# Seven products instead of eight for the first product of chunk 7 and half of chunk 8 of a fused attention and MoE kernel, its gate on GpSimd, x and w_in in fp16

## The chip, the cores and the metric

The kernel runs on one core of one Trainium2 chip. Its engines are TensorE (PE, with its weight loads as PEld), VectorE (DVE), ScalarE (ACT), GpSimd (POOL) and SyncE (SP, which here only issues DMAs). The metric is the device time of one execution in microseconds, the median of several; lower is better.

## The reference

Block-wise causal attention for 8 batches and 8 heads, 576 positions of 64 numbers each, and behind it a two-layer network with a gate. Inputs and output are float32.

```python
scores = scale * np.matmul(q, k.transpose(0, 1, 3, 2))      # scale = 1/8
mask = block_i >= block_j                                   # blocks of 64 positions
attn = softmax(where(mask, scores, -1e9))
x = (attn @ v).transpose(0, 2, 1, 3).reshape(B * S, H * D)  # 4608 x 512
h = x @ w_in                                                # 512 x 2048
g = h * (1.0 / (1.0 + np.exp(-beta * h)))
return g @ w_out                                            # 2048 x 512
```

## The kernel before

**Who decides the order.** The kernel is written as a list of operations (`P.op`), each with the engines that may run it, an estimated duration, what it depends on, the buffers ("tiles") that it holds, and a priority. When the program is made, `Plan.schedule` runs these through a list scheduler: whenever an engine is free it takes, among the operations whose dependencies have ended by the estimates and for which buffers are free, the one with the lowest `prio`. The result is a fixed order for every engine's queue; on the chip each engine works its queue in that order and waits on semaphores. The estimates are `mm(n)` for a matmul of n columns, `act_t(n)` for ScalarE, `dve_t(n)` for VectorE, and plain numbers for GpSimd. PSUM has eight banks of 512 float32 columns; a "P1" tile is one bank, a "PP" tile (attention) a pair.

**Attention.** For each batch and each pair of heads: q and k are loaded (SP queue), cast to bf16 on GpSimd (L625, L665), transposed (PE at L634, later by DMA), multiplied (L708), put through Exp on ScalarE (L724, L736), zeroed where masked (VectorE, L730, L732) and multiplied with v (L764; v is cast on GpSimd at L574). VectorE divides by the row sums into `xq` (L776, L783), and `xq` is transposed into `xT`, by PE and a copy for the first three batches (L813, L821, L823) and by DMA for the rest (L800). `xT` holds x transposed, four blocks of 128 features by up to 2560 rows, in bf16, used as a ring.

**The network.** It goes over nine chunks of 512 rows (r = 0 to 8; chunk 7 begins at row 3584, chunk 8 at 4096). Each chunk has two products.

The first product (L1000) makes 16 blocks of 128 hidden units: for block j four matmuls, over the four blocks of features, of 128x128 weights from `w_in` on 512 columns of `xT`, into one bank. ScalarE takes tanh of it with the scale beta/2 (L1010), and VectorE forms (tanh + 1) times h from the same bank into `gT` in fp16 (L1014), which is 2 h sigmoid(beta h); the factor 2 is taken out at the end.

```python
o = P.op("PE", 4 * mm(512), fh, deps=xd + [win[j // 4]], tiles=[ph, tg], lat=4 * mm(512) + 170,
         mode="full", prio=1000 + 100 * r + j)
```

The second product is, for chunks 1 to 8 (`FAST`), already done in seven products instead of eight (Strassen's way, Winograd's form): `gT` is seen as 2x2 quarters (row half by half of the hidden units), `w_out` likewise, and sums and differences of quarters are multiplied (`fast`, L921, 128x256 matmuls in fp16). VectorE makes these sums (L885, two SBUF inputs; those of `w_out` once, L865). Three of the results run through one bank: ScalarE copies it out (L942), the next product adds into the same bank, and so on; VectorE adds the other banks (L945, and L936 in the last chunk). The outputs go to DRAM through the ACT queue, in the last chunk through SP.

The priorities interleave the second product of chunk r with the first product of chunk r+1: its first two steps stand behind the first product of its own chunk, and the others between the blocks of the next chunk.

```python
prio=1000 + 100 * r + (16 + 0.1 * k if fin or k < 2 else 103 + 16 / 12 * (k - 2))
```

`gT` has two buffers, so the first product of chunk r+1 can begin when the second product of chunk r-1 has ended. Chunk 8 has nothing behind it: its second product runs alone.

**Buffers.** Most of SBUF is taken. The staging buffers of q and k (`ST`, `S4`), of v (`Vs`), the cast copies (`QKn`, `Vn`), the transposed ones (`QKT`) and the exponentials (`E`) are used until the attention of the last batch is done.

**Start.** GpSimd builds two 128x128 identities (L458 to L463), constants in `Vn` and `E`, and then turns to the casts and to the loads of `w_in` and `w_out`, which convert from float32 on the way (L502, L507). Until 50 us TensorE fills pauses with matmuls on constants (L523, L525).

Of the kernel before, what the change touches and what calls it, by code (L numbers as in the profile page):

```python
# [4 lines left out]
ACT = mybir.ActivationFunctionType  # L5
ALU = mybir.AluOpType
f32 = mybir.dt.float32
# [6 lines left out]
NF = 2048  # L14
# [345 lines left out]
def bass_blockwise_causal_attn__then__act_swish_beta_kernel(  # L360
# [10 lines left out]
    with es:  # L371
        def sb(name, shape, dt):
            return es.enter_context(nc.sbuf_tensor(name, shape, dt))
# [7 lines left out]
        JOIN = (2,3,4,5,6,7)  # L381
        NO = 4
        FAST = range(1, NRC)
        RX = 5 * RC
        OV = sb("OV", [128, 5120], f32)
        ST = [sb(f"ST{i}", [128, 36, 64], f32) for i in range(2)]
        STh = [s[:, 18 * i:18 * i + 18] for s in ST for i in range(2)]
        ST6 = [s[0:96].rearrange("p t d -> p (t d)")[:, 768 * i:768 * i + 768].rearrange("p (h j d) -> p h j d", h=2, j=6)
               for s in ST for i in range(3)]
        Vs = [sb("Vs0", [128, 5, 8, 64], f32), OV[:, 2560:5120].rearrange("p (t h d) -> p t h d", t=5, h=8)]  # L390
        OVh = OV[:].bitcast(f16).rearrange("p (s j n) -> p s j n", s=5, j=8)
        TW = {k: OVh[:, k - 2] for k in (2, 3, 4)}
        SW = {k: OVh[:, k + 1] for k in (2, 3)}
        QKn = [sb(f"QKn{i}", [128, 2, 2, 768], bf16) for i in range(NQ)]
        Vn = [sb(f"Vn{i}", [128, 5, 8, 66], bf16) for i in range(NQ)]
        QKT = [sb(f"QKT{i}", [128, 2, 2, 640], bf16) for i in range(3)]
        Ef = [sb(f"E{i}", [128, 3200], bf16) for i in range(NE)]
        gT = [sb(f"gT{i}", [128, NJ, RC], f16) for i in range(2)]

        Ef.append(gT[1][:].bitcast(bf16).rearrange("p j n -> p (j n)")[:, 0:3200])  # L400
        E3 = [e[:, 0:3072].rearrange("p (c h n) -> p c h n", c=3, h=2) for e in Ef]
        E4 = [e[:, 3072:3136] for e in Ef]
        inv = [sb(f"inv{i}", [128, 10], f32) for i in range(4)]
        xq = [sb(f"xq{i}", [128, 5, 128], bf16) for i in range(3)]
        xq.append(gT[1][:].bitcast(bf16).rearrange("p j n -> p (j n)")[:, 3200:3840].rearrange("p (i n) -> p i n", i=5))
        xT = sb("xT", [128, 4, RX], bf16)
        identF = sb("identF", [128, 128], f32)
        identB = sb("identB", [128, 128], bf16)
        w_in = sb("w_in", [128, 4, NF], bf16)
        w_out = sb("w_out", [128, NJ, DM], f16)  # L410
        beta = sb("beta", [128, NJ], f32)
        th = [sb(f"th{i}", [128, RC], f32) for i in range(3)]
# [3 lines left out]
        PS = es.enter_context(nc.psum_tensor("PS", [128, 8, 512], f32))  # L416
        PSb = PS[:].rearrange("p b n -> p (b n)").bitcast(bf16).rearrange("p (b n) -> p b n", b=8)

        identW = identF[:].bitcast(bf16)
        NFILL, TFILL = 400, 50000.0  # L420
        P = Plan()
# [2 lines left out]
            P.slots(c, n)  # L424
        P.slots("S4", 4)
        P.slots("XX", 1)

        def mm(n):
            return max(n / 2.4 + 3, 55.0)

        def act_t(n, ptr=0):
            return 0.833 * n + 93 + 93 * ptr

        def dve_t(n):
            return (n + 125) / 0.96

        LAG = 1.5
        def pr(u):
            b, c = divmod(u, NPAIR)
            return u if b < 1 else 10 * u if b < 2 else 994 + 100 * (b - LAG) + 4.9 * c  # L440
# [11 lines left out]
        def xq_(tx):  # L452
            return 3 if tx.cls == "XX" else tx.slot

        def mk(fn):
            return lambda g, e: fn(g)
# [6 lines left out]
        c4 = P.op("POOL", 430, mk(lambda g: g.affine_select(  # L463
            out=identB[:], in_=identB[:], compare_op=ALU.not_equal, fill=1.0, base=0,
            pattern=[[-1, 128]], channel_multiplier=1)), deps=[c3], prio=-10)
        c2.same, c4.same = [c1], [c3]
        cw = P.op("POOL", 100, mk(lambda g: g.memset(warm[:, 0:1], 0.0)), prio=-20)
        wa = P.op("ACT", 1500, mk(lambda g: g.activation(warm[:, 1:2], warm[:, 0:1], ACT.Exp)), deps=[cw], prio=-60)
        ones, vzero = [], []
# [131 lines left out]
        for u in range(NU):  # L601
# [208 lines left out]
            def fx(g, e, tx=tx, px=px):  # L810
                for i in range(5):
                    r = 128 if i < 4 else 64
                    z = g.transpose(PSb[:, px.slot, 128 * i:128 * i + r], xq[xq_(tx)][0:r, i, :], identB[0:r, 0:r])  # L813
                return z

            xp = P.op("PE", 5 * 66, fx, deps=nrm, tiles=[tx, px], lat=5 * 66 + 170, mode="full", prio=pr(u)+.5 + 5 * (b < 1))

            def fy(g, e, px=px, c=c, b=b):
                for t0, n, x0 in pieces(b):
                    if e == "ACT":  # L820
                        z = g.activation(xT[:, c, x0:x0 + n], PSb[:, px.slot, t0:t0 + n], ACT.Copy)  # L821
                    else:
                        z = g.tensor_copy(xT[:, c, x0:x0 + n], PSb[:, px.slot, t0:t0 + n])  # L823
                return z
            xt.append(P.op("ACT" if u in (2, 3) else "DVE", 600 if u in (2, 3) else 520, fy, deps=[xp], tiles=[px], prio=0))

# [44 lines left out]
        def fast(r, row, tg, gs):  # L871
# [114 lines left out]
            else:  # L986
                store(ou, 1, 0, evac(Y, ou, p4 + [u2], add=ou), rest=1500.0 if r < NRC - 2 else 0.0)

        for r in range(NRC):
            row = RC * r  # L990
            b0, b1 = row // S, (row + RC - 1) // S
            xd = [xt[4 * b + c] for b in range(b0, b1 + 1) for c in range(4)]
            tg = P.tile("gT")
            gs, hs = [], []
            for j in range(NJ):
                ph, tt = P.tile("P1"), P.tile("th")

                def fh(g, e, ph=ph, j=j, row=row):
                    for c in range(4):
                        z = g.matmul(PS[:, ph.slot, :], w_in[:, c, 128 * j:128 * j + 128], xT[:, c, row % RX:row % RX + RC],  # L1000
                                     start=(c == 0), stop=(c == 3))
                    return z

                o = P.op("PE", 4 * mm(512), fh, deps=xd + [win[j // 4]], tiles=[ph, tg], lat=4 * mm(512) + 170,
                         mode="full", prio=1000 + 100 * r + j)

                hs.append(o)

                def fs(g, e, ph=ph, tt=tt, j=j):
                    return g.activation(th[tt.slot][:], PS[:, ph.slot, :], ACT.Tanh, scale=beta[:, j:j + 1])  # L1010
                a = P.op("ACT", act_t(512, 1), fs, deps=[o, bC], tiles=[ph, tt], lat=act_t(512, 1) + 93, prio=0)

                def fg(g, e, ph=ph, tt=tt, tg=tg, j=j):
                    return g.scalar_tensor_tensor(out=gT[tg.slot][:, j, :], in0=th[tt.slot][:], scalar=1.0,  # L1014
                                                  in1=PS[:, ph.slot, :], op0=ALU.add, op1=ALU.mult)
                gs.append(P.op("DVE", dve_t(512), fg, deps=[a] + (spare.users + spare_x.users if r == 1 else []), tiles=[ph, tt, tg], prio=0))

            for b in range(B):
                if any((S * b + a) // RC - RX // RC == r for a in (0, S - 1 if b < XB else 639)):
                    for c in range(4):  # L1020
                        xt[4 * b + c].deps += hs

            if r in FAST:
                fast(r, row, tg, gs)
                continue

            for w, d0, d1 in [(w, 0, DM) for w in range(4)]:
                po, to = P.tile("P1"), P.tile("ost")


                parts = [(4 * a, 4 * a + 4) for a in range(4)]
                o = None
                for j0, j1 in parts:
                    def fo(g, e, po=po, tg=tg, w=w, j0=j0, j1=j1, d0=d0, d1=d1):
                        for j in range(j0, j1):
                            z = g.matmul(PS[:, po.slot, 0:d1 - d0], gT[tg.slot][:, j, 128 * w:128 * w + 128],  # L1036
                                         w_out[:, j, d0:d1], start=(j == 0), stop=(j == NJ - 1))
                        return z

                    n = (j1 - j0) * mm(d1 - d0)  # L1040
                    was = o
                    o = P.op("PE", n, fo, deps=gs[j0:j1] + wout[j0 // 4:(j1 + 3) // 4],
                             tiles=[po, tg], lat=n + 170, mode="full",
                             prio=1000 + 100 * r + (16 + w + 0.01 * j0 if w == 0 else
                                                     103 + 5.33 * (w - 1) + 1.33 * j0 / 4))
                    o.after = was
                    plain.append(o)

                def fv2(g, e, po=po, to=to, n=d1 - d0):
                    if e == "ACT":  # L1050
                        return g.activation(ost[to.slot][:, 0:n], PS[:, po.slot, 0:n], ACT.Copy, scale=0.5)
                    return g.tensor_scalar(out=ost[to.slot][:, 0:n], in0=PS[:, po.slot, 0:n], scalar1=0.5,
                                           scalar2=None, op0=ALU.mult)
                x = P.op("ACT", act_t(d1 - d0) + 80, fv2, deps=[o], tiles=[po, to], lat=act_t(d1 - d0) + 160, prio=0)

                def fd(g, e, to=to, row=row, w=w, d0=d0, d1=d1):
                    return [g.dma_start(out[row + 128 * w:row + 128 * w + 128, d0:d1], ost[to.slot][:, 0:d1 - d0])]
                P.op("ACT", 500, fd, deps=[x], tiles=[to], xfer=900, dma=["d_ost", to], prio=-1)
# [71 lines left out]
```

The softmax here doesn't subtract the row's maximum and nothing guards it: scores larger than these inputs give would overflow.

## Time and profile before

| what | value |
|---|---|
| runs | 334.65, 335.12, 332.92 us; median 334.65 |
| span of the profiled execution, first to last instruction | 330.9 us |
| TensorE, matmuls | 323.5 us busy, 98% |
| VectorE, ScalarE, GpSimd | 221.8, 212.6 and 84.6 us busy |
| first product (L1000) | 576 matmuls |
| second product by seven (L921) | 896 matmuls |
| granted TensorE clock, mean | 0.999 |
| last attention matmul (L764) ends | 262.1 us |
| chunk 7's first product | 267.3 to 288.0 us, mixed with chunk 6's second |
| chunk 8's first product | 292.5 to 314.2 us, mixed with chunk 7's second |
| chunk 8's second product | 314.2 to 328.2 us |

The profiled execution's time is known by its span only; the times of the runs also hold what lies around it, so they stand 2.0 to 4.2 us above the span. A row of the profile gives line, engine, operation, output and inputs, count, then busy time and the mean of one in ns, and last the idle time of the engine before such operations with what ended it. Matmuls overlap, so that the mean of one is longer than its share of the time. In the chain that ended last a piece is given by its start, its length and the instructions in it. In the table of stretches the columns are start and end, length, then busy time and count of PE, PEld, DVE, ACT and POOL, the granted clock, and the DMAs.

### The profile page before, as it was taken

To read this page: it belongs to the slowest core of one execution; us is meant where nothing else is said; L and a number is where in the kernel's file an instruction comes from. 1 tells how busy PE (TensorE), PEld (TensorE's weight loads), DVE (VectorE), ACT (ScalarE), POOL (GpSimd) and SP (SyncE) were. 2 spreads that over 40 slices of the span, in tenths; PEclk is the share of its full clock that TensorE was granted. 3 is DMA by queue.
4 is the path that set the end of the run, shared out by engine and by line. 5 is a ranking of instruction groups with operands and counts; after the bars stand their busy time and mean duration, and the time that the engine had idled before them with its cause. 6 is when DMAs were issued, how large, how long until landed. Compare 5 with 4: busy or idle time off the path is not lost.

```text
span 330.9 us, 7510 instructions
## 1 busy us (share of the span) xinstructions
PE 323.5 (98%) x3145; PEld 204.2 (62%) x3089; DVE 221.8 (67%) x448; ACT 212.6 (64%) x324; POOL 84.6 (26%) x127
## 2 busy tenths in 40 slices
PE   7998999999999999999999999999999999999996
PEld 4574455445586457754765666576566766666685
DVE  4747875679754897358966695678467685666742
ACT  2876974297558886768657866974975555544521
POOL 7665081073073044104621530320000000000000
PEclk9999999999999999999999999999999999999999
DMA  7999999999999999979999999974102310110023
GB/s 214 229 239 234 192 234 198 187 293 200 202 268 190 207 247 198 229 158 216 204 176 224 199 240 214 200 152 80 35 34 40 92 45 34 60 37 32 3 95 127
DMA packets 154993, 53.41 MB, mean 161 GB/s; under 512 B 139072, under 2 KB 154448, under 8 KB 154960
## 3 DMA queue, kind: packets, MB, share of 16 engines
q1 hardware_dynamic: 141200, 40.19, 63.9%
q0 software_dynamic: 5568, 4.36, 8.3%
q10 hardware_dynamic: 8192, 8.39, 8.1%
q8 instruction: 24, 0.39, 0.5%
q14 instruction: 9, 0.07, 0.1%
HBM read 36.71 MB, written 9.44 MB: 139 GB/s over the span
## 4 chain that ended last, share of the span: by engine, by line
PE 92%; ACT 2%; DMA 2%; issue 1%; DVE 1%; SPq 1%; POOL 0%
PE PS L1000 38%; PE PS L921 30%; PE PS L708 9%; PE PS L764 8%; PE PS L1036 4%; DMA ST<-in_k_dram 2%; PE PS L525 1%; PE PS L813 1%; ACT E L724 1%; PE PS L634 1%; ACT xq L788 1%; SPq L618 1%; ACT th L1010 0%; POOL QKn L625 0%; DVE xq L783 0%
## 5 line engine op out<-in xcount | busy, mean ns | idle before, releaser
L1000 PE MATMUL PS<-xT,w_in 128*128 128x512 bf16 x576 | 136.6, 379 | 0.1
L1010 ACT ACTIVATE th<-PS,beta 128x512 f32<-128x512 f32 x144 | 96.5, 699 | 59.8 <-PE PS L1000 59.1
L1014 DVE SCALAR_TENSOR_TENSOR gT<-th,PS 128x512 f16<-128x512 f32 x144 | 95.1, 681 | 31.7 <-ACT th L1010 31.1
L724 ACT ACTIVATE E<-PS 128x1024 bf16<-128x1024 f32 x93 | 92.1, 1028 | 27.0 <-PE PS L708 27.0
L1000 PEld LDWEIGHTS PS<-xT,w_in 128*128 128x128 bf16 x576 | 53.4, 98 | 55.5 <-DVE gT L1014 1.8
L921 PE MATMUL PS<-w_out,gT 128*128 128x256 f16 x512 | 63.1, 273 | 0.0
L921 PEld LDWEIGHTS PS<-w_out,gT 128*128 128x128 f16 x512 | 49.0, 98 | 12.1 <-issue 1.5
L574 POOL CAST Vn<-Vs 128x640 bf16<-128x640 f32 (+1 forms) x28 | 21.6, 770 | 94.3 <-DMA Vs<-in_v_dram 93.1
L665 POOL CAST QKn<-ST 128x640 bf16<-128x640 f32 x48 | 36.7, 764 | 25.1 <-DMA ST<-in_q_dram 12.9
L708 PE MATMUL PS<-QKT 64*128 64x320 bf16 (+4 forms) x328 | 36.4, 297 | 0.4 <-ACT E L736 0.2
L764 PEld LDWEIGHTS PS<-Vn,E 128*128 128x128 bf16 x930 | 30.9, 97 | 3.9 <-issue 0.4
L942 ACT ACTIVATE ost<-PS 128x512 f32<-128x512 f32 x32 | 19.4, 606 | 21.5 <-PE PS L921 21.5
L921 PE MATMUL PS<-OV 128*128 128x256 f16 x256 | 31.9, 273 | 0.0
L764 PE MATMUL PS<-Vn,E 128*128 128x65 bf16 x930 | 31.8, 193 | 0.0
L708 PEld LDWEIGHTS PS<-QKT 64*128 64x128 bf16 (+1 forms) x328 | 13.4, 96 | 26.4 <-issue 11.6
L921 PEld LDWEIGHTS PS<-OV 128*128 128x128 f16 x256 | 24.2, 98 | 5.8 <-issue 1.1
L783 DVE TENSOR_TENSOR xq<-PS,inv 128x640 bf16<-128x640 f32 x30 | 24.6, 822 | 0.7
L885 DVE TENSOR_TENSOR OV<-gT 128x1024 f16<-128x1024 f16 x32 | 23.8, 753 | 1.1 <-PE PS L921 0.6
L730 DVE MEMSET E<- 64x64 uint32 x62 | 6.9, 112 | 22.5 <-ACT E L724 20.4
L945 DVE SCALAR_TENSOR_TENSOR ost<-PS,ost 128x512 f32<-128x512 f32 x22 | 15.1, 688 | 8.7 <-PE PS L921 6.2
L921 PE MATMUL PS<-OV,gT 128*128 128x256 f16 x128 | 16.1, 273 | 0.0
L1036 PE MATMUL PS<-w_out,gT 128*128 128x512 f16 x64 | 15.5, 380 | 0.0
(65 smaller groups left out, 176.2 us busy)
## 6 DMA issues: line engine op xcount, KB each, us to landing
out_dram<-ost ACTq DMA_DIRECT2D x32, 256.0 KB, 3.8
ST<-in_q_dram SPq DMA_DIRECT2D x12, 576.0 KB, 5.4
ST<-in_k_dram SPq DMA_DIRECT2D x12, 576.0 KB, 7.6
Vs<-in_v_dram SPq DMA_DIRECT2D x24, 256.0 KB, 4.3
ST<-in_q_dram SPq DMA_DIRECT2D x8, 288.0 KB, 6.3
ST<-in_k_dram SPq DMA_DIRECT2D x8, 288.0 KB, 6.5
w_in<-in_moe_w_in_dram POOLq DMA_DIRECT2D x4, 512.0 KB, 10.5
w_out<-in_moe_w_out_dram POOLq DMA_DIRECT2D x4, 512.0 KB, 9.5
```

The costliest lines, as they stand in the source:

```text
L574: return g.tensor_copy(Vn[t.slot][:, 0:n, g0:g1, 0:64], Vs[ts.slot][:, 0:n, g0:g1, :])
L665: return g.tensor_copy(QKn[tn.slot][:].rearrange("p a w n -> p (a w n)")[:, 640 * (2 * a + w):][:, 0:640] .rearrange("p (t h d) -> p t h d ...
L708: z = g.matmul(o, QKT[tqk.slot][r, uu % 2, 1, 128 * t + y:128 * t + m + y], x)
L724: return g.activation(E3[es_(te)][:, g0, :, :], PS[:, ps.slot:ps.slot + 2, :], ACT.Exp, scale=0.125)
L764: z = g.matmul(o, eblk(te, t, i, h), Vn[Tv.slot][:, t, 2 * c + h, 0:65], start=(t == 0), stop=(t == i))
L783: return g.tensor_tensor(xq[xq_(tx)][:].rearrange("p i (h d) -> p h i d", h=2), both(pv, 0, 64), x, ALU.mult)
L885: return P.op("DVE", dve_t(SZ * HC / 2), mk(lambda g: g.tensor_tensor(fo(), fx(), fy(), op)), deps=deps, tiles=tiles, prio=prio)
L921: x = g.matmul(PS[:, pw.slot, HM * w:HM * w + HM], fa()[:, j, 128 * w:128 * w + 128], fb()[:, j, :], start=first and (pair or w == 0) and ...
L1000: z = g.matmul(PS[:, ph.slot, :], w_in[:, c, 128 * j:128 * j + 128], xT[:, c, row % RX:row % RX + RC], start=(c == 0), stop=(c == 3))
L1010: return g.activation(th[tt.slot][:], PS[:, ph.slot, :], ACT.Tanh, scale=beta[:, j:j + 1])
L1014: return g.scalar_tensor_tensor(out=gT[tg.slot][:, j, :], in0=th[tt.slot][:], scalar=1.0, in1=PS[:, ph.slot, :], op0=ALU.add, op1=ALU.mult)
L1036: z = g.matmul(PS[:, po.slot, 0:d1 - d0], gT[tg.slot][:, j, 128 * w:128 * w + 128], w_out[:, j, d0:d1], start=(j == 0), stop=(j == NJ - 1))
```

## The change

For chunk 7 (all 16 blocks of hidden units) and chunk 8 (blocks 0 to 7) the first product, too, is done in seven products instead of eight, by a new function `first`. A group is four blocks f: two neighbours i = 0, 1 from each half of eight blocks (chunk 7's groups 0 and 2 cover blocks 0 to 7, groups 4 and 6 blocks 8 to 15). x is seen as 2x2 quarters (256 rows by 256 features), w_in of the group likewise (256 features by 256 hidden units). Each of the seven products has four matmuls of 256 columns.

- Sums and differences of quarters of `w_in` are made once, on GpSimd (`first_weights`, eight operations of 128x1024 in fp16, priority 500, after the last cast of q and k). Those of x are made by VectorE at the beginning of each of the two chunks (four operations).
- The results are put together in float32 in SBUF (`C4`): ScalarE copies a bank out three times a group (`copy`), VectorE adds three banks (`plus`) and copies one. Each holds 2h. Both the combined tiles and those behind them lie in buffers that the attention has used (`ST`, `Vs`, `QKn`, `Vn`, `E`, `QKT`), so chunk 7's products wait for the attention's last use of them.
- The gate becomes ScalarE's Sigmoid from SBUF into `TH` (seven buffers), and a multiplication of `TH` with `C4` on GpSimd into `gT`. The other blocks keep Tanh and the gate on VectorE.
- x (`xq`, `xT`) and `w_in` are fp16 instead of bf16; the transposes on PE need a third identity, in fp16, which GpSimd builds at the start.

```diff
+        F1 = {7: (0, 2, 4, 6), 8: (0, 2)}
...
-        xT = sb("xT", [128, 4, RX], bf16)
+        xT = sb("xT", [128, 4, RX], f16)
...
-        w_in = sb("w_in", [128, 4, NF], bf16)
+        identH = sb("identH", [128, 128], f16)
+        w_in = sb("w_in", [128, 4, NF], f16)
...
+        for c, n in (("T4", 2), ("C4", 9), ("TH", 7)):
+            P.slots(c, n)
...
+        c5 = P.op("POOL", 260, mk(lambda g: g.memset(identH[:], 0.0)), prio=-3)
+        c6 = P.op("POOL", 430, mk(lambda g: g.affine_select(
+            out=identH[:], in_=identH[:], compare_op=ALU.not_equal, fill=1.0, base=0,
+            pattern=[[-1, 128]], channel_multiplier=1)), deps=[c5], prio=-3)
...
+        def first_weights():
+            old = users("ST", "S4") + win
+            a = [[A(f, k) for k in range(2)] for f in range(2)]
+            for k, x, y, op, d in ((1, a[1][0], a[1][1], ALU.add, ()), (3, a[0][0], a[1][0], ALU.subtract, ()),
+                                   (2, SI[1], a[0][0], ALU.subtract, (1,)), (4, a[0][1], SI[2], ALU.subtract, (2,))):
+                si[k] = []
+                for c in range(2):
+                    z = P.op("POOL", 2400, mk(lambda g, o=SI[k], x=x, y=y, c=c, op=op: g.tensor_tensor(
+                        o[:, c], x[:, c], y[:, c], op)), deps=old + [q for i in d for q in si[i]], prio=500)
...
+        def first(r, row, tg, xd):
...
+            dead = users("QKn", "QKT", "Vs", "V", "E") if r == min(F1) else []
...
+                t[k] = P.op("DVE", 400, mk(lambda g, k=k, a=a, b=b, op=op: g.tensor_tensor(TX[tx.slot][k], a(), b(), op)),
+                            deps=xd + dead + [t[i] for i in d], tiles=[tx], prio=0.4)
...
+            for j in F1[r]:
+                Z, W, Y = (P.tile("P1") for _ in range(3))
+                ca, cb = P.tile("C4"), P.tile("C4")
+                at = [1000 + 100 * r + 2 * j]
+
+                def prod(ps, fa, fb, deps, tiles, start, j=j):
+                    def f(g, e):
+                        for i in range(2):
+                            for c in range(2):
+                                z = g.matmul(PS[:, ps.slot, 256 * i:256 * i + 256],
+                                             fa()[:, c, j // 4, 128 * (j % 4 + i):128 * (j % 4 + i) + 128], fb()[:, c, :],
+                                             start=start and i == 0 and c == 0, stop=i == 1 and c == 1, skip_group_check=True)
...
+                    n = 4 * mm(256)
+                    o = P.op("PE", n, f, deps=deps, tiles=[ps, tg, *tiles], lat=n + 170, mode="full", prio=at[0])
+                    at[0] += 0.5
...
+                p1 = prod(Z, lambda: A(0, 0), lambda: X(0, 0), xd + win + dead, [], True)
+                z1 = copy(Z, ca, 0, [p1])
+                p2 = prod(W, lambda: A(0, 1), lambda: X(1, 0), [p1], [], True)
+                c11 = plus(W, ca, 0, [p2, z1])
+                p7 = prod(Y, lambda: SI[3], lambda: TX[tx.slot][3], [t[3], *si[3]], [tx], True)
+                p6 = prod(Z, lambda: SI[2], lambda: TX[tx.slot][2], [t[2], *si[2], z1], [tx], False)
+                u2 = copy(Z, cb, 0, [p6])
+                p5 = prod(Z, lambda: SI[1], lambda: TX[tx.slot][1], [t[1], *si[1], u2], [tx], False)
+                u4 = copy(Z, cb, 1, [p5])
+                c22 = plus(Y, cb, 1, [p7, u4])
+                p3 = prod(Z, lambda: SI[4], lambda: X(1, 1), [u4, *si[4]], [], False)
+                c12 = P.op("DVE", dve_t(512), lambda g, e, Z=Z, ca=ca: g.tensor_scalar(
+                    out=C4[ca.slot][:, :, 1], in0=pair(Z), scalar1=2.0, scalar2=None, op0=ALU.mult),
+                           deps=[p3], tiles=[Z, ca], prio=0)
+                p4 = prod(Y, lambda: A(1, 1), lambda: TX[tx.slot][4], [t[4], c22, *win], [tx], False)
+                c21 = plus(Y, cb, 0, [p4, u2])
+                for i in range(2):
+                    for f, c, d in ((j + i + j // 4 * 4, ca, [c11, c12]), (j + i + j // 4 * 4 + 4, cb, [c21, c22])):
+                        tt = P.tile("TH")
+                        a = P.op("ACT", act_t(512, 1), lambda g, e, tt=tt, f=f, c=c, i=i: g.activation(
+                            TH[tt.slot], C4[c.slot][:, i].rearrange("p h n -> p (h n)"), ACT.Sigmoid, scale=beta[:, f:f + 1]),
+                            deps=d + [bC], tiles=[c, tt], lat=act_t(512, 1) + 93, prio=0)
+                        gs[f] = P.op("POOL", 1250, lambda g, e, tt=tt, f=f, c=c, i=i: g.tensor_tensor(
+                            gT[tg.slot][:, f, :], TH[tt.slot], C4[c.slot][:, i].rearrange("p h n -> p (h n)"), ALU.mult),
+                            deps=[a, *d], tiles=[c, tt, tg], prio=0)
...
-            for j in range(NJ):
+            if r in F1:
+                gs, hs = first(r, row, tg, xd)
+            for j in [j for j in range(NJ) if gs[j] is None]:
```

## The prediction

> **What bounds the kernel now.** I began with the page: engine shares, the forty slices, the chain that ended last.
>
> ```profile
> span 330.9 us, 7510 instructions
> ...
> PE 323.5 (98%) x3145; PEld 204.2 (62%) x3089; DVE 221.8 (67%) x448; ACT 212.6 (64%) x324; POOL 84.6 (26%) x127
> ...
> POOL 7665081073073044104621530320000000000000
> ...
> PE 92%; ACT 2%; DMA 2%; issue 1%; DVE 1%; SPq 1%; POOL 0%
> ```
>
> TensorE is the bound: it works 98% of the span, it is 92% of the chain, and the change touches stretches in which it never pauses. GpSimd has nothing to do in the last 110 us. A microsecond of TensorE work removed near the end is therefore a microsecond of time, but only if the other engines deliver no later than before.
>
> Next the pieces of the chain (start, length, what), because a matmul's own mean includes overlap with the next one, and only back-to-back runs give its true rate:
>
> ```profile
> 267.32 5.18 PE PS L1000 x24
> ...
> 314.16 13.99 PE PS L921 x128
> ```
>
> A 512-column matmul of the first product takes 5.18/24 = 0.216 us, a 256-column matmul of the second product 13.99/128 = 0.1093 us. Two of the small ones cost 0.219, so halving the width costs 1%, although each has its own weight load (98 ns by the L921 row, hidden beneath the matmul).
>
> Then the stretches of chunk 7's and chunk 8's first products (us, then PE, weight load, DVE, ACT, POOL busy):
>
> ```profile
> 262.95:288.12 25.17, 25.17 (x170) 16.39 (x169) 17.82 (x28) 13.39 (x20) 0.00 (x0) 1.00 0.10 29
> 288.12:314.16 26.04, 26.04 (x178) 17.24 (x177) 17.59 (x27) 13.39 (x20) 0.00 (x0) 1.00 0.12 41
> 314.16:330.90 16.74, 13.97 (x128) 12.20 (x126) 6.17 (x11) 3.08 (x5) 0.00 (x0) 0.99 0.32 111
> ```
>
> TensorE is full in the first two, ScalarE half busy, GpSimd empty. The third is chunk 8's second product, alone; the change leaves it as it is.
>
> **The change, part by part.**
>
> *Matmuls.* Four blocks of 128 hidden units took 16 matmuls of 512 columns, 16 x 0.216 = 3.45 us. They become seven products of 4 matmuls of 256 columns, 28 x 0.1093 = 3.06 us. That saves 0.39 us a group; chunk 7 has four groups and chunk 8 two, so 6 x 0.39 = **2.36 us** at the most. The 28 weight loads take 28 x 0.098 = 2.74 us, still under the matmuls. fp16 for bf16 changes no size: the fp16 rate above is the bf16 rate for twice the columns. The transposes, copies and casting loads that now carry fp16 keep their bytes, so I cost them at nothing.
>
> *ScalarE.* Rows for the operations that a group will use:
>
> ```profile
> L1010 ACT ACTIVATE th<-PS,beta 128x512 f32<-128x512 f32 x144 | 96.5, 699 | 59.8 <-PE PS L1000 59.1
> ...
> L942 ACT ACTIVATE ost<-PS 128x512 f32<-128x512 f32 x32 | 19.4, 606 | 21.5 <-PE PS L921 21.5
> ...
> L945 DVE SCALAR_TENSOR_TENSOR ost<-PS,ost 128x512 f32<-128x512 f32 x22 | 15.1, 688 | 8.7 <-PE PS L921 6.2 <-ACT ost L942 2.3
> ```
>
> A group had four tanhs, 4 x 0.70 = 2.80 us; it gets three copies out of PSUM and four sigmoids, 3 x 0.61 + 4 x 0.70 = 4.61. Chunk 7 adds 4 x 1.82 = 7.3 us to ScalarE's 13.4, so 20.7 us in a stretch that should shrink to 25.2 - 1.6 = 23.6: 88% full. Chunk 8 adds 3.6, 17 of 25. Both fit, chunk 7 barely. What hides the copies is other TensorE work: ten steps of chunk 6's second product (10 x 0.87 = 8.7 us), the neighbouring group, and later chunk 8's plain blocks.
>
> *A table load.* ScalarE loads a table once, at the start, and then serves exp and tanh from it:
>
> ```profile
> L468 ACT ACT_TABLE_LOAD x1 | 1.3, 1283 | 0.8 <-PEq L1115 0.8
> ```
>
> Sigmoid is nowhere in this trace. If that table holds it too, the price is 0; if not, one load of 1.28 us before chunk 7's first sigmoid; if chunk 8's tanhs then need the old table back, 1.28 us more at each return. The nearest row is one load serving several functions, so I take one, **1.28 us**. The plan that fixes every engine's order doesn't know of it, and behind it in ScalarE's queue stand the next group's copies, for which TensorE waits with the next product.
>
> The Trainium skill speaks against this step: its page "ScalarE: Activation LUTs", section "Table sets: the hidden batching unit", puts sigmoid into a set without exp (but with tanh), and "What ACT_TABLE_LOAD costs" adds a drain of about 1.38 us, 2.66 in all; by it the sum below would be 1.4 us worse, and no returns would follow. The row shows only the 1283 ns.
>
> *GpSimd.* It gets 24 gates (two SBUF inputs, 128x512 f32) and eight combinations of w_in (128x1024 f16). No two-input operation of GpSimd is in the trace. Its nearest row is the cast:
>
> ```profile
> L665 POOL CAST QKn<-ST 128x640 bf16<-128x640 f32 x48 | 36.7, 764 | 25.1 <-DMA ST<-in_q_dram 12.9 <-DMA ST<-in_k_dram 10.1
> ```
>
> 764/640 = 1.19 ns an element for one input. If a second input costs nothing, a gate takes 512 x 1.19 = 0.61 us; if the inputs are read in turn, 1.22. And casts slow down beside a VectorE operation with two SBUF inputs (L885), and slow that one too. This is the stretch from 163 to 168 us, GpSimd's answer first and VectorE's below it:
>
> ```profile
> L665 POOL CAST QKn<-ST 128x640 bf16<-128x640 f32 x4 | 4.0, 992 | 3.1 <-DMA ST<-in_q_dram 2.6 <-DMA ST<-in_k_dram 0.3
> ...
> L885 DVE TENSOR_TENSOR gT<-gT,OV 128x1024 f16<-128x1024 f16 x2 | 2.2, 1128 | 0.0
> ```
>
> 992 ns for 764, and 1128 for a median of 686. Read in turn and always so crowded, a gate takes 1024 x 992/640 = 1.59 us. I take 1.22, since two operands through an engine that takes 1.19 ns for one is nearest, and add the crowding separately: eight L885 operations in each chunk, each costing GpSimd about 0.25 us ((4.0 - 3.0)/4), 2 us a chunk.
>
> The w_in combinations begin after GpSimd's last cast (218.5 us). At two reads of 1024 elements they are 8 x 2.4 = 20 us, at one 10, at the crowded rate 25; done by 229 to 244, long before chunk 7 at 267. That idle time hides them; without it they would delay the third of seven products.
>
> For the gates the room decides. The first can start when a whole group has gone through its chain: four products of 0.44 with 0.18 of latency each (the idle time that ScalarE's tanhs show behind a matmul), three copies of 0.61 with about 0.2, one VectorE pass, one sigmoid: 2.5 + 2.4 + 0.9 + 0.9 = 6.7 us after 267.2, so at 273.9, with the table load at 275.2. Chunk 8's second product reads the last of them at 314.0 - 2.4 = 311.6. That is 36.4 us for 24 gates, 1.52 each. At 1.22 and 4 us of crowding they take 33: it fits, with 3 us to spare.
>
> The order of instructions, however, is fixed when the program is made, at a planned 1.25 us a gate and no crowding. TensorE's first step that needs chunk 7's sixteen gates stands where the plan has them ready, so lateness there is a wait. I estimate 16 x (1.22 - 1.25) + 2.0 = 1.5 us of lateness, of which GpSimd's gaps between the groups' bursts absorb about half: **0.6 us** of wait (bounds: -0.3 with no crowding, 5.4 at 1.59).
>
> The Trainium skill's "GPSIMD Engine Reference", section "Performance versus the Vector engine", advises against the move as well: elementwise work with two inputs belongs on VectorE, which is about twice as fast; its 2.6 cycles an element at 1.2 GHz make an estimate of 1.11 us a gate, 24 of them 27 us instead of 29, and the wait would be nothing.
>
> *VectorE.* A group had four gates of 0.68; it gets three additions (0.69) and one scaled copy (at most 0.69), the same 2.7 us. Four differences of x (128x512 f16, half of L885's 0.69 to all of it) add 1.4 to 2.8 us a chunk to 17.8 of 25: no cost, and only the products three to seven wait for them.
>
> *The head.* A third identity is built on GpSimd, a memset and a select of 0.20 and 0.29 us (as for identB). They may stand before the first cast, which starts at 5.2 us: 0 to 0.6 us late, taken at 0, because TensorE fills that time with 34 and 74 matmuls on constants.
>
> **Sum.** -2.36 + 1.28 + 0.6 = -0.5 us. The profiled span is 330.9; the median of the runs is 334.65, 3.75 above it (the lowest run 2.0), and I take what lies around the span as unchanged. Forecast: 334.65 - 0.5 = **334.2 us**.
>
> **Rivals.**
>
> A. *TensorE never waits.* The table load falls into ScalarE's spare 12% and the gates keep their plan: 334.65 - 2.36 = **332.3**. For it: TensorE has no pause from 262 to 328 us under the same kind of plan. Against: the load is not in the plan. With luck in the new order a little lower.
>
> B. *GpSimd becomes the bound of the last 45 us*, the slower side. Place: the gates; price: beyond 1.52 us a gate, 24 times the excess, and before that the lateness against 1.25. At 1.59, twenty-four gates are 24 x 0.34 = 8.2 us late, less the 3 us of gaps: 334.65 - 2.36 + 1.28 + 5.2 = **338.8**. It decides from about 1.35 us a gate with crowding (16 x 0.1 + 2 = 3.6 us late eats the whole gain). For it: the crowded rows and no gate in the trace. Against: crowding has been only part of the time, 48 casts average 764.
>
> C. *The round trips.* Each group returns one PSUM bank to TensorE three times through ScalarE, in whose queue sigmoids stand in bursts of four. If every copy of chunk 7 waits for one sigmoid and half of that is uncovered, 12 x 0.7 / 2 = 4.2 us: 334.65 - 2.36 + 4.2 = **336.5**. Against: there are 8.7 us of other products and a neighbouring group to run meanwhile.
>
> **How the numbers follow.** Chances: forecast 0.45 (332.8 to 336), A 0.17, B 0.22, C 0.16. The range 331.8 to 340.0 goes from A with some luck to past B. About 1% (3.3 us) is what a measurement of this kernel can tell from no change. Faster by more than that needs more than the 2.36 us that exist: 0.06. Slower by more (over 338.0) is most of B and a third of C: 0.24. Within: 0.70.
>
> **What would show it.** Right: L921-like matmuls in the first product at 0.109 us; a second table load of about 1.28 us near 273; gates at 1.2 to 1.4 us, with the longer ones beside L885; pauses of TensorE of 1 to 3 us in total, at the second group and at the first step that needs chunk 7's upper gates; the last stretch still 16.7 us. Wrong: gates above 1.5, TensorE waiting for gT again and again, several table loads, or pauses before the attention has ended.

## The result, and the profile after

The changed kernel takes 338.97 us (median; 338.50 to 339.82), the kernel before 333.94 beside it: ratio 1.0145, interval 1.0109 to 1.0180. It is slower by 5 us where a gain of 0.5 was forecast. The measured time lies in the forecast's range, on the other side of zero. Single runs of one kernel differ by some us, the longer ones mostly at a granted clock of 0.995 or less, so below each kernel is judged by its ratio to the runs of before that were made with it. Differences in us are of medians; where the ratios give another figure it stands beside.

The page of the changed kernel, the lines that answer to those shown of before:

```profile
span 336.8 us, 7748 instructions
...
PE 323.8 (96%) x3219; PEld 210.3 (62%) x3163; DVE 230.6 (68%) x456; ACT 221.6 (66%) x343; POOL 138.5 (41%) x161
...
PE 78%; DVE 8%; POOL 5%; ACT 4%; DMA 2%; issue 1%; SPq 1%; POOLq 0%
```

TensorE is no longer the whole chain: VectorE holds 8% of it and GpSimd 5%, where before they had 1% and 0. The profiled execution took 338.68 us, 1.9 above its span; the profiled one of before stands 5.9 us lower in span.

Who made TensorE wait (what waited, for whom, us in total, times, longest):

```profile
PE PS L947 <- DVE OV L911: 2.7, 2, 2.5
...
PE PS L947 <- POOL gT L1111: 1.9, 2, 1.3
```

The first of these lies near 237 us, in the second product of an earlier chunk that the change doesn't touch. These are three stretches of the changed kernel (columns as in the table of before):

```profile
237.00:262.00 25.00, 22.51 (x247) 14.19 (x242) 17.57 (x36) 17.23 (x27) 4.41 (x2) 1.00 0.10 25
262.00:288.00 26.00, 25.95 (x241) 21.74 (x238) 18.85 (x36) 16.41 (x28) 6.92 (x6) 1.00 0.22 55
288.00:314.00 26.00, 23.79 (x197) 18.60 (x195) 19.52 (x28) 16.16 (x28) 21.27 (x15) 1.00 0.12 42
```

TensorE idles 2.5 us before chunk 7 begins, almost nothing while most of chunk 7's first product runs, and 2.2 us from 288 to 314, where GpSimd is busy 21 of 26 us. To find where the 5.9 us went I took the distance from each matmul's start to the next one's, less the usual distance for its shape, and summed this by stretch, after against before. The head (to the first matmul of the first product) is 1.1 us later, 50 to 214 us loses about 0.5, 214 to 262 us 3.3, and from 262 us on it is 3.5. Together 8.4; less the 2.4 us that the smaller products save, 6.0.

Near 237 us it happens like this. VectorE (first fence) and GpSimd (second), each line a start, a length and what ran:

```profile
229.82 2.10 DVE L911 TENSOR_TENSOR gT<-gT 128x1024 f16<-128x1024 f16 x1
231.84 1.87 DVE L1143 SCALAR_TENSOR_TENSOR gT<-th,PS 128x512 f16<-128x512 f32 x3
233.63 0.82 DVE L911 TENSOR_TENSOR OV<-gT 128x1024 f16<-128x1024 f16 x1
234.38 2.61 DVE L911 TENSOR_TENSOR gT<-gT 128x1024 f16<-128x1024 f16 x1
237.02 2.49 DVE L911 TENSOR_TENSOR OV<-gT 128x1024 f16<-128x1024 f16 x1
```

```profile
222.63 8.74 POOL L1032 TENSOR_TENSOR SA<-w_in 128x1024 f16<-128x1024 f16 x4
231.45 4.99 POOL L1032 TENSOR_TENSOR SA<-SA,w_in 128x1024 f16<-128x1024 f16 x2
236.52 4.97 POOL L1032 TENSOR_TENSOR SA<-w_in,SA 128x1024 f16<-128x1024 f16 x2
```

While GpSimd makes the w_in combinations, three of VectorE's four sums for the second product (L911 after, L885 before: 0.69 us) take 2.1 to 2.6 us, about one GpSimd instruction. The first of them ends at 231.92, 0.55 us after the GpSimd instruction that it had met (222.63 + 8.74 = 231.37), as if it had begun only then. The fourth, which met the end of one, took 0.82. The gates between them (L1143, one input in PSUM) keep their 0.6 us. TensorE's next product, at 239.56, waits for that last sum.

### The profile page after: what moved, and what is told of

The parts are those of the page before. It is cut to its first block, busy times and chain, and to the rows that moved or that the text cites. A ratio compares the mean times of both kernels' runs of the same rounds, so it can differ in the third digit from the quotient of the medians.

```text
span 336.8 us, 7748 instructions
## 1 busy us (share of the span) xinstructions
PE 323.8 (96%) x3219; PEld 210.3 (62%) x3163; DVE 230.6 (68%) x456; ACT 221.6 (66%) x343; POOL 138.5 (41%) x161
## 4 chain that ended last, share of the span: by engine, by line
PE 78%; DVE 8%; POOL 5%; ACT 4%; DMA 2%; issue 1%; SPq 1%; POOLq 0%
PE PS L1129 28%; PE PS L947 24%; PE PS L734 8%; PE PS L790 8%; POOL gT L1111 5%; PE PS L1165 4%; DVE gT L911 2%; DMA SA<-in_k_dram 2%; DVE OV L911 2%; DVE gT L1143 2%; PE PS L1066 2%; PE PS L839 1%; PE PS L551 1%; ACT QT L1108 1%; ACT EA L750 1%
## 5 line engine op out<-in xcount | busy, mean ns | idle before, releaser
L1129 PE MATMUL PS<-xT,w_in 128*128 128x512 f16 x480 | 115.1, 380 | 0.8 <-issue 0.5
L750 ACT ACTIVATE EA<-PS 128x1024 bf16<-128x1024 f32 x93 | 92.1, 1027 | 25.5 <-PE PS L734 24.0
L1143 DVE SCALAR_TENSOR_TENSOR gT<-th,PS 128x512 f16<-128x512 f32 x120 | 78.2, 680 | 15.7 <-ACT th L1139 15.1
L1129 PEld LDWEIGHTS PS<-xT,w_in 128*128 128x128 f16 x480 | 43.5, 98 | 46.8 <-issue 2.8
L600 POOL CAST VA<-Vs 128x640 bf16<-128x640 f32 (+1 forms) x28 | 20.3, 723 | 95.4 <-DMA Vs<-in_v_dram 94.1
L947 PEld LDWEIGHTS PS<-w_out,gT 128*128 128x128 f16 x512 | 48.8, 98 | 13.9 <-DVE gT L1143 1.9
L691 POOL CAST QA<-SA 128x640 bf16<-128x640 f32 x48 | 39.0, 812 | 26.6 <-DMA SA<-in_k_dram 14.3
L734 PE MATMUL PS<-QT 64*128 64x320 bf16 (+4 forms) x328 | 36.4, 297 | 0.2 <-ACT EA L750 0.2
L968 ACT ACTIVATE ost<-PS 128x512 f32<-128x512 f32 x32 | 19.2, 600 | 23.4 <-PE PS L947 23.4
L790 PEld LDWEIGHTS PS<-VA,EA 128*128 128x128 bf16 x930 | 30.9, 97 | 4.4 <-issue 0.4
L790 PE MATMUL PS<-VA,EA 128*128 128x65 bf16 x930 | 31.8, 193 | 0.0
L911 DVE TENSOR_TENSOR OV<-gT 128x1024 f16<-128x1024 f16 x32 | 27.7, 868 | 1.9 <-POOL gT L1111 0.8
L809 DVE TENSOR_TENSOR xq<-PS,inv 128x640 f16<-128x640 f32 x30 | 24.6, 821 | 0.6
L911 DVE TENSOR_TENSOR gT<-gT 128x1024 f16<-128x1024 f16 x16 | 15.4, 962 | 2.1 <-POOL gT L1111 2.0
```

The lines of the kernel that those rows point to most:

```text
L600: return g.tensor_copy(Vn[t.slot][:, 0:n, g0:g1, 0:64], Vs[ts.slot][:, 0:n, g0:g1, :])
L691: return g.tensor_copy(QKn[tn.slot][:].rearrange("p a w n -> p (a w n)")[:, 640 * (2 * a + w):][:, 0:640] .rearrange("p (t h d) -> p t h d ...
L734: z = g.matmul(o, QKT[tqk.slot][r, uu % 2, 1, 128 * t + y:128 * t + m + y], x)
L750: return g.activation(E3[es_(te)][:, g0, :, :], PS[:, ps.slot:ps.slot + 2, :], ACT.Exp, scale=0.125)
L790: z = g.matmul(o, eblk(te, t, i, h), Vn[Tv.slot][:, t, 2 * c + h, 0:65], start=(t == 0), stop=(t == i))
L809: return g.tensor_tensor(xq[xq_(tx)][:].rearrange("p i (h d) -> p h i d", h=2), both(pv, 0, 64), x, ALU.mult)
```

## The experiments

Times are medians; the ratio is to the kernel before in the same session.

**Only the types (e1).** `F1` is emptied.

```diff
-        F1 = {7: (0, 2, 4, 6), 8: (0, 2)}
+        F1 = {}
```

> No group is done by seven products (F1 empty), so the w_in combinations, the copies, the sigmoids and the gates on GpSimd are gone; fp16 and the third identity stay. Theory (three separate losses: the third identity delays the head by 0.6 to 1.1 us; the w_in combinations on GpSimd hold up VectorE's two-input sums and cost 3.0 us of TensorE waits near 237 us; the stretches of chunks 7 and 8 lose about 1): 1.1 us above before, 335.0. Rival 'the gates are the bound and nothing else costs': as before, 333.9. Rival 'fp16 or the rearranged buffers cost by themselves': 337 or more.

Measured 335.85, ratio 1.0045 (1.0018 to 1.0072): 1.5 us are lost with no group at all. The reason could be seen at GpSimd's start, here of the changed kernel:

```profile
5.13 0.21 POOL L488 MEMSET identH<- 128x128 f16 x1
5.49 0.29 POOL L489 TENSOR_SCALAR_AFFINE_SELECT identH<-identH 128x128 f16<-128x128 f16 x1
5.92 0.82 POOL L651 CAST QA<-SA 96x768 bf16<-96x768 f32 x1
```

The first cast began at 5.20 us before and begins at 5.92 now, behind the third identity.

**Types and an identity that comes later (e12).** It waits for the load of the third pair's k.

```diff
         win[0].deps += [ld["K", 0]]
+        c5.deps.append(ld["K", 2])
```

> As e1 (no groups, fp16 and the third identity), but the identity is built in GpSimd's gap near 14 us. Theory 'the identity before the first cast is e1's loss at the head': 0.6 to 1.4 us below e1, 334.5 to 335.2, at most 0.4 us above before. Rival 'another order of the head or fp16 itself': as e1, 335.9.

Measured 335.09, ratio 1.0010 (0.9984 to 1.0036). The loss is gone to within the error; the two intervals just overlap, so the identity is the likely cause and not a proven one. (The order of instructions on TensorE, VectorE and ScalarE is the same in both; only GpSimd's differs.) fp16 itself costs nothing that these runs can measure. The same edit in the whole change (e4):

> The whole change, but the third identity waits for a later load (k of the third pair), so that GpSimd builds it in its gap near 14 us, after the first casts. Theory: 0.6 to 1.1 us below the changed kernel, 338.1, and the first product begins at 28.2 us as before in place of 29.3. Rival 'the head is slack': 339.0, no difference.

Measured 338.43, ratio 1.0144 (1.0092 to 1.0196): no difference that shows. Its trace is 1.2 us shorter (span 335.6) and its median 0.5 us, but the ratio is the same.

**The w_in combinations alone (e2).** `F1` is empty, and `first_weights()` is called once ahead of the loop over chunks.

> As e1, but GpSimd makes the eight combinations of w_in at their place, and nobody reads them. Theory: 3.0 us above e1, 338.0, with VectorE's two-input sums at 2 to 2.6 us beside them and a pause of TensorE of 2.5 us near 237. Rival 'the gates alone': the same as e1 to 0.5 us, since TensorE has other work.

Measured 338.88, ratio 1.0147 (1.0109 to 1.0185), 3.0 us above e1 (3.4 by the ratios). So work that nobody reads, on an engine that was idle, costs as much as the whole change. TensorE's longest wait is again 2.5 us for an L911 sum. The other engines' queues have the same order in e1, e2 and the next run, so that only GpSimd's work differs.

**The same in pieces (e8).**

```diff
-                    z = P.op("POOL", 2400, ... o[:, c], x[:, c], y[:, c], op ...
+                    for n in range(4):
+                        z = P.op("POOL", 600, ... o[:, c, q, w], x[:, c, q, w], y[:, c, q, w], op ...
```

> As e2 (no groups, the w_in combinations made on GpSimd and read by nobody), but each combination is made in four pieces of 256 elements, 32 instructions of about 0.6 us. Theory 'VectorE's two-input sum waits until GpSimd's instruction has ended': its longest drops from 2.5 to at most 1.4 us, and the time falls by about 2 us, to 336.5. Rival 'the two share a port's rate': the sums stay at 2 us or more and the time at 338.9.

Measured 335.52, ratio 1.0018 (0.9981 to 1.0054), 3.4 us below e2 (4.3 by the ratios, in two sessions). First e2's sums by duration (min/median/max in ns), then those of e8, then e8's pieces:

```profile
L911 DVE TENSOR_TENSOR OV<-gT x32: 677/692/2486, 69.8 to 322.7; 128x1024 f16<-128x1024 f16 x32
L911 DVE TENSOR_TENSOR gT<-gT x16: 629/692/2636, 79.0 to 322.0; 128x1024 f16<-128x1024 f16 x16
```

```profile
L911 DVE TENSOR_TENSOR OV<-gT x32: 679/692/1242, 71.5 to 321.0; 128x1024 f16<-128x1024 f16 x32
L911 DVE TENSOR_TENSOR gT<-gT x16: 630/692/1209, 80.7 to 320.3; 128x1024 f16<-128x1024 f16 x16
```

```profile
L1033 POOL TENSOR_TENSOR SA<-w_in x16: 667/672/1076, 225.8 to 238.4; 128x256 f16<-128x256 f16 x16
```

GpSimd does the same work in more time (32 x 0.67 = 21 us at least, where eight whole ones took 18.7), yet VectorE's worst falls from 2.64 to 1.24. A port shared by rate would not care for the pieces. What counts is how long one GpSimd instruction lasts.

**The w_in combinations on VectorE**, in the whole change (e3), and then with the late identity as well (e5):

```diff
-                    z = P.op("POOL", 2400, ...
+                    z = P.op("DVE", dve_t(512), ...
```

> The whole change, but VectorE makes the eight combinations of w_in (8 x 0.69 us) in place of GpSimd. Theory: 3.0 us below the changed kernel, 336.0, no VectorE two-input operation over 1.2 us before 262 us. Rival 'the gates alone': 339, or later still by VectorE's 5.5 us more work.

> The whole change with the w_in combinations on VectorE and the third identity in GpSimd's gap near 14 us. Theory (the gates on GpSimd take back in chunks 7 and 8 what the other two moves give): 336.9 to 337.6, and TensorE still waits 3 to 4 us for gT between 288 and 315 us. Rival 'the losses add up independently': 338.97 - 3.0 - 0.6 = 335.4.

Measured 338.17 (1.0107; 1.0051 to 1.0163) and 338.87 (1.0108; 1.0037 to 1.0180). The pause near 237 us is gone, but both are only about 1.2 us below the changed kernel by the ratios, so that more than half of its price comes back: VectorE, with 5.5 us more work there, delivers its own gates later (1.0 us of TensorE's time in e5, 0.2 in e3), and in both TensorE's waits for GpSimd's gates grow to 3.0 us. This is e5's line:

```profile
PE PS L948 <- POOL gT L1113: 3.0, 2, 1.7
```

**Pieces and late identity in the whole change (e11)**, the gates left as they are:

> The whole change with only the third identity late and the w_in combinations on GpSimd in pieces of 256. Theory: as e5, since the gates are what is left: 337.5, 2 to 4 us of waits for gT, 3.5 us or so above e9. Rival 'without the pause near 237 the rest fits': 335.

Measured 336.47, ratio 1.0050 (1.0022 to 1.0078). That is 2.5 us below the changed kernel (3.2 by the ratios), more than e5 gave. Its waits for gT are 1.9 us in two pieces, as in the changed kernel.

**Gates of half the length (e7)**, in the order of e5:

```diff
-   gT[tg.slot][:, f, :], TH[tt.slot], C4[c.slot][:, i].rearrange("p h n -> p (h n)"), ALU.mult)
+   gT[tg.slot][:, f, 0:256], TH[tt.slot][:, 0:256], C4[c.slot][:, i, 0], ALU.mult)
```

> As e5, in the same order of instructions, but each gate on GpSimd multiplies only the first 256 of its 512 columns (the other half of gT keeps old values). Theory: the waits of TensorE for gT vanish, 3 to 4 us below e5: 333.5. Rival 'the round trips through ScalarE hold TensorE': no lower than 336.5, with TensorE waiting for copies.

Measured 335.27, ratio 1.0006 (0.9964 to 1.0048), 3.6 us below e5 with the same queues. Its stretches:

```profile
262.00:288.00 26.00, 26.00 (x264) 21.55 (x263) 20.29 (x38) 17.58 (x31) 6.13 (x8) 1.00 0.14 34
288.00:314.00 26.00, 26.00 (x214) 20.71 (x212) 20.79 (x32) 20.09 (x34) 12.96 (x17) 1.00 0.12 42
```

TensorE is full again and waits for no gate of GpSimd. (It lost 2.0 us earlier, near 214 to 241 us, to VectorE's gates behind the combinations, as e5 lost 1.0; the gain from the gates is rather larger than 3.6.) The round trips through ScalarE, which stand in both, make it wait for none of their copies. The gates are the bound, by their own time on GpSimd or by what they hold up on VectorE; the next run tells which.

**Each gate in two halves, both done (e14).** GpSimd then holds VectorE for a shorter time, but needs longer for the sum.

> As e11 (whole change, identity late, w_in combinations in pieces), but each gate is two instructions of 256 columns, in the same order. Theory 'the waits for gT are GpSimd's own time': 24 gates at 1.34 us in place of 1.27 stay late, waits for gT of 2 us or more, 336.5 to 337. Rival 'the gates cost through VectorE, which they hold': 2 us below e11, 334.5.

Measured 340.85, ratio 1.0192 (1.0143 to 1.0241), 4.4 us above e11: the theory's side, but far above its 336.5 to 337. The halves, and TensorE's waits:

```profile
L1113 POOL TENSOR_TENSOR gT<-QT,QA x24: 723/727/1231, 283.0 to 325.2; 128x256 f16<-128x256 f32 x24
```

```profile
PE PS L948 <- POOL gT L1113: 5.1, 3, 1.8
```

Two halves take 1.45 us (forecast 1.34) where one gate took 1.27, and the waits rise from 1.9 to 5.1, though VectorE's longest sum falls from 1.76 to 1.25. So in chunks 7 and 8 it is GpSimd's own throughput that TensorE waits for, more than the hold on VectorE. (Its profiled execution is the longest of the six and lost 2.0 us more in one wait for a transposing DMA; the median doesn't hang on it.)

**Half of the gates on VectorE (e9).**

```diff
-  gs[f] = P.op("POOL", 1250, lambda ...
+  od = i == 1
+  gs[f] = P.op("DVE" if od else "POOL", 691 if od else 1500, lambda ...
```

> All six groups, the third identity late, the w_in combinations on GpSimd in pieces of 256, and of each group's four gates two on VectorE (planned at 0.69 us) and two on GpSimd (planned at 1.5). Theory (twelve gates no longer bound TensorE): the waits for gT between 288 and 315 us fall below 1 us, and the time is 333.5, a little under before. Rival 'a VectorE gate has two SBUF inputs and waits out GpSimd's': VectorE's gates at 1.5 us or more, waits of 2 us or more, 336.5.

Measured 337.03, ratio 1.0065 (1.0035 to 1.0094): near the rival. The waits for GpSimd's gates are gone, as the theory had it, but TensorE now waits three times 0.9 us for VectorE. VectorE's own gates have two inputs in SBUF; the twelve took 13.9 us in all, where 0.69 us each would make 8.3, and six of them were:

```profile
L1114 DVE TENSOR_TENSOR gT<-QT,QA x6: 677/1163/1767, 279.2 to 313.3; 128x512 f16<-128x512 f32 x6
```

That they wait out GpSimd's gates is the likely reason; what the added work alone costs was not run.

**No second table (e6).** Tanh stands in place of Sigmoid.

> As e5, but ScalarE takes Tanh in place of Sigmoid, so no second table is loaded; the gate's factor is then another function than the reference's, and only the time is read. Theory 'the gates' own length': 0 to 0.6 us below e5, the waits for gT hardly change. Rival 'the unplanned table load shifts all gates': 1.3 us below e5, with the waits for gT smaller by as much.

Measured 338.71, ratio 1.0090 (1.0046 to 1.0134), against e5's 1.0108: 0.2 us below e5 at the median, 0.6 by the ratios. The waits for gT are 2.2 us in place of 3.0, which lies between the two forecasts. Whatever the table load costs, these runs do not resolve it.

**Four groups.** Only groups 0 and 2 of each chunk, with the late identity and the pieces (e10); then with each gate in two halves (e13); then that in bf16 (e15).

> Only groups 0 and 2 of chunks 7 and 8 by seven products, all their gates on GpSimd (planned at 1.5 us), the third identity late, the w_in combinations in pieces. Theory: 16 gates over two chunks fit into GpSimd's time, 4 x 0.39 = 1.6 us saved less 0.5 at the head: 333.7, waits for gT below 1 us. Rival 'any gate on GpSimd is late for its reader': 2 us of waits again, 336.

> As e10 (four groups), but each gate on GpSimd is two instructions of 256 columns. Theory 'VectorE is held for one GpSimd instruction at a time': VectorE's two-input sums at most 1.4 us beside gates (1.66 in e10), TensorE's waits in chunks 7 and 8 fall from 0.7 to below 0.3 us; 334.1, 0.4 below e10, under before by 0.5 to 1. Rival 'no effect': 334.5.

> As e13, but x, w_in and their sums stay in bf16, so there is no third identity; the output is then rounded more coarsely. Theory 'the head's rest comes with the identity': 0.3 to 0.7 us below e13, 333.6, clear of before by about 1 us. Rival 'no difference of types': 334.1.

Measured 334.51 (1.0008; 0.9979 to 1.0037), 335.26 (1.0024; 0.9997 to 1.0051) and 336.89 (1.0051; 1.0016 to 1.0085). The first is the best version found: 4.5 us better than the change as it was made, level with the kernel before, and not better than it. Of the 4 x 0.39 = 1.6 us that it saves, TensorE gives back 0.7 in chunks 7 and 8 (by the start-to-start distances). Halved gates were expected to help and did not: TensorE waits 1.1 us for gT in e13 and not at all in e10, though VectorE's longest sum falls from 1.66 to 1.23 us. (Its gates were planned at 1.4 us in place of 1.5, which orders the queues differently, so that the halves alone are not compared.) The bf16 version was expected to be the fastest and has the highest median of the three. Its runs (334.76 to 338.33, and one of 344.67) overlap those of e13 (334.16 to 337.40), and so do the intervals, so that no difference of types is shown either way. Its trace shows 2.3 us of waits for gT and 2.0 us at the start, and its queues are ordered differently throughout; I can't say why beyond that.

## Why the prediction was wrong, point by point

*Matmuls*: right. The first product's small matmuls start 109 ns apart (L1066, the usual distance), 512-column ones 216, in fp16 as in bf16, which makes the 0.39 us a group. No run shows the saving by itself.

*The w_in combinations*: here the prediction failed first. "done by 229 to 244, long before chunk 7 at 267. That idle time hides them" was right on when GpSimd would finish (241.5 us) and wrong on who else would pay. Their durations lie inside the bounds (2.13 alone, 2.45 beside VectorE). What was not costed is VectorE: the crowded row had shown 1128 ns in place of 686 beside casts of 0.76 us, and I carried only GpSimd's side of it into the sum. The excess is not a factor; it grows with the length of the GpSimd instruction. Read as "waits for up to one instruction", the row would have given 0.69 + 2.1 = 2.8 us beside a combination, and such a sum stands ahead of a product. Price: 0 in the sum, 3.0 us measured (e2 against e1), 3.4 given back by pieces (e8 against e2; 3.4 and 4.3 by the ratios).

*The gates*: right in mechanism, wrong in size. A gate takes 1.27 us alone and 1.78 at most beside a two-input sum, close to the 1.22 plus crowding that I took (the other estimate, 1.11, is further off). The wait behind them was put at 0.6 us; from 262 us on TensorE loses 3.5 (the stretches; e7 against e5 gives 3.6), 2.3 of it directly behind gates. GpSimd's side of chunk 7, its sixteen gates:

```profile
280.62 8.10 POOL L1111 TENSOR_TENSOR gT<-QT,QA 128x512 f16<-128x512 f32 x6 [39.13 <-ACT QT L1108]
288.80 6.33 POOL L1111 TENSOR_TENSOR gT<-QT,VA 128x512 f16<-128x512 f32 x4
295.21 8.84 POOL L1111 TENSOR_TENSOR gT<-QT,EA 128x512 f16<-128x512 f32 x6
```

They took 23.4 us, where the plan had 16 x 1.25 = 20.0: 3.4 us more, and I had estimated 1.5. The crowding was as estimated (1.8 us, estimated at 2.0); the gates' own time was 20.4 in place of 19.5, and 0.08 us or a little more between one gate and the next, 1.3 in all, was not in the sum. And "GpSimd's gaps between the groups' bursts absorb about half" failed: there were no gaps, GpSimd ran one gate after another until 304.1, and TensorE's first step that needs all of them came at 304.2. (Half of 1.5 would also have been 0.75 and not 0.6.) The first gate started at 280.6, not at 275.2: chunk 7's products began at 271.2 in place of 267.2, which moves the gates' readers as well (in e11 they began 1.0 us earlier, with the same 23.4 us and the same 1.9 us of waits), and the group's chain, with the table load, took 9.4 us in place of 8.0, which does not. In this part rival B named the right bound, and its condition, 1.35 us a gate with crowding, was met (1.41 on average); its 338.8 is near the measured time by luck, from another sum: it had the gates at 1.59 us and no other loss.

*The table load*: happened as I took it, one load, none for the tanhs that follow. Its price of 1.28 us in the sum can't be made out: TensorE doesn't pause at it, and e6 gains 0.2 us at the median. Up to 0.8 us of it may reach TensorE through the gates, whose waits are shorter by that in e6.

```profile
278.53 1.28 ACT L1108 ACT_TABLE_LOAD   x1
279.82 1.33 ACT L1108 ACTIVATE QT<-QA,beta 128x512 f32<-128x512 f32 x2
```

The sigmoid starts where the load ends, and the copy ahead of the load had ended where it starts (277.92 + 0.60). The drain that the Trainium skill's page "ScalarE: Activation LUTs" adds ("What ACT_TABLE_LOAD costs") can't be seen here; the same page's sets ("Table sets: the hidden batching unit") are borne out, since a load stood ahead of the first sigmoid and one load served sigmoid and the later tanhs.

*The head*: "taken at 0, because TensorE fills that time" was wrong. The first cast came 0.7 us late, just past the bounds given (0 to 0.6). TensorE fills the time because it has nothing to do, and what it waits for there comes later by as much. The first matmul of the first product came at 29.3 us in place of 28.2; e1 against e12 puts 0.8 us on it, with wide intervals.

*The base*: the changed kernel's profiled execution lies 1.9 us above its span, so the profiled one of before took about 332.8 us, a quick one, and about half of the 3.75 us that I added was spread of the runs. That moves the level and not the difference.

*ScalarE's round trips* (rival C): refuted by e7, which keeps them all and waits for none. *VectorE's load* was right in work (18.9 to 19.5 us busy in the two stretches) and wrong in what it leaves out, as above.

The terms by the runs: -2.4 for the products, 3.0 to 3.4 for the w_in combinations, 3.5 for the gates, 0.8 to 1.5 for the head make 4.9 to 6.0; measured 5.0. The saving and the head are the less certain of these terms.

## What to carry to other kernels

Idle time of an engine is not free when its instructions hold up those of a busy one: before moving two-input work to GpSimd, look for VectorE instructions with two SBUF inputs in the same stretch, price each at one whole GpSimd instruction, and cut the GpSimd work into short pieces. Then ask who waits for the delayed instruction in the fixed order of the queues, also in stretches that the change doesn't touch. Where an engine is to take work at a rate near its limit, the time of its first operation and the pause between two of them count beside the length of one: a chain of dependent round trips ahead of it eats the room, and no gaps are left to catch up in.

## What the runs showed of the hardware that I had not expected

A two-input elementwise instruction on GpSimd holds a VectorE instruction with two SBUF inputs for up to the rest of its own length: sums of 0.69 us took up to 2.64 beside instructions of 2.13 us, up to 1.76 beside gates of 1.27, up to 1.24 beside pieces of 0.67. GpSimd loses only 0.3 to 0.5 us each time. VectorE's gates with one input in PSUM keep their time (680 ns). The Trainium skill's page "GPSIMD Engine Reference" ("Key points") names the contention and, as one of two conditions, two SBUF inputs; how long it lasts here, and that VectorE pays the larger part, these runs show.

A gate of 512 columns costs GpSimd 1.27 us and one of 256 columns 0.73, so by these two sizes some 0.18 us of each instruction doesn't depend on its size; cutting instructions shorter is right where another engine is held (e8) and wrong where GpSimd itself is the bound (e14).
